# A state-space layer with a gated feed-forward: filter spectrum kept on chip with an exchanged copy, stages of two time steps, twiddles from a sine table, an explicit order

## The chip, the cores and the metric

The kernel runs on one core of a Trainium2 chip. A core has TensorE (matrix products, results into PSUM), VectorE (DVE), ScalarE (ACT), GpSimd (POOL) and SyncE (SP), which run side by side and meet at semaphores, and 16 DMA engines that move data between the memory off the core and SBUF. SP and ACT each have a queue from which they issue transfers; a queue issues in order, so an issue that waits holds up all that stand behind it. The metric is device time in microseconds, median of the runs.

## The reference

With S = 2048 time steps, D = 512 channels and F = 1792:

```python
xn = layernorm(A_q)                                     # over D
k_shift[t] = sum_j A_k[t - j] * shift_k[:, j]           # 4 taps
kv = k_shift * A_v
y  = irfft(rfft(kv, 2S) * rfft(ssm_k, 2S))[:S] + kv * ssm_D   # long convolution, per channel
s  = xn * y
h  = gelu(xn @ w_gate) * (xn @ w_up)
g  = silu(h @ w_down)
out = A_q + s * g
```

All inputs and the output are bfloat16. Two parts are independent until the end: the feed-forward (gate, up, down), and the long convolution, a product of two spectra of 4096 points.

## The kernel before

**Time steps.** A row of 128 partitions times 16: partition p holds time steps 16p to 16p + 15, and "row t" is the 128 steps with the same remainder t. `X` holds the input, `XN` the normalised input, `G` the gate and later the output, each 16 rows of 128 x 512.

**Feed-forward.** Four groups q of four rows. `ln(q)` (L857) takes statistics on DVE, a power on GpSimd and normalises on DVE; `xn_transpose(q)` (L882) brings channels to the partitions (`xnT`), by TensorE for q = 0 and by a DMA transpose on SP for the others. `unit(q, m)` (L1151) is one slice of 128 of the 1792 columns: four gate matmuls, four up matmuls of 512 columns, gelu on ACT (`GE`), product on DVE (`HT`). `down(q)` (L1178) is 14 matmuls a row, then tanh and a multiply into `G`, or silu in the last group.

**Convolution.** An FFT of two stages, each a matrix product, with the data regrouped through memory off the core between them.
- `h_transpose` (L917) turns the filter to time steps on the partitions (`HTr`) in 64 TensorE transposes of 128 x 128. `kshift` (L1026) computes the four taps on DVE into `V`.
- `stage1` (L999): row t against `F1[:, t]`, a table of cosines and sines that holds the first stage and the twiddle factors of row t together; two matmuls, one eviction of 128 x 1024 on ACT, one store of 256 KB to ZH (filter) or ZK (data). Filter evictions go to `ASH`, eight buffers inside `G`.
- `table` (L775), `phase`, `sins` make `F1`: 16 iotas on GpSimd, an addition and a mask on DVE, sines on ACT, each of 128 x 1024 in four parts. `G1`, its transpose, serves the last stage and is made by four DMA transposes (L1102). The second-stage matrices `MT` (three of 128 x 128) are made by some fifteen small operations (L960 to L989) and a sine, which needs ACT's table switched twice.
- `h_stage2(n)` (L1076), n = 0 to 7: loads 512 KB of ZH as `BH`, 16 matmuls on tiles of 32 x 32 (`tiles`, L1061; here a *set*), two evictions, and two stores of 256 KB to ZS.
- `spectrum(n)` (L1115): loads the filter spectrum from ZS into `HS` in two forms, so that real and imaginary parts stand at both places (two loads of 512 KB), loads `BK` from ZK, a forward set, two evictions to `KB`, four products on DVE into `HB` and `KS`, two inverse sets into one PSUM pair, two evictions to `BO` (two buffers), two stores to ZI, issued by ACT.
- At L1226 the last stage: 16 loads `BI` of 256 KB, four matmuls for two rows against `G1`, a multiply out of PSUM.

**Order.** `Sched.run` (L384) simulates the engines with assumed durations and picks, whenever an engine is free, the ready task of the lowest priority number (the `P_` constants) among those that could start within a small slack; PSUM banks and buffers are handed out on the way. Instructions are then issued in that order on each engine, and `Trk` puts in the semaphore waits. Input loads come first on SP, in the order of the string `ORDER`.

Of the kernel before, what the change touches and what calls it, by code (L numbers as in the profile page):

```python
# [14 lines left out]
DM = 512  # L15
# [8 lines left out]
N_WARM = 11  # L24
ORDER = ("w1 k0 v0 w2 k1 v1 w3 x1 d0 d1 k2 v2 k3 v3 x2 x3", "w1 k0 v0 w2 x1 k1 v1 w3 d0 d1 k2 v2 k3 v3 x2 x3",
         "w1 k0 v0 w2 k1 w3 v1 x1 d0 d1 k2 v2 x2 k3 v3 x3", "w1 k0 v0 w2 k1 v1 w3 d0 x1 d1 k2 v2 k3 v3 x2 x3")[int(0.2)]
NF_BANKS = 4
ISSUE = 470.0
NC_PAIRS = 4
SMALL = 1.15 * 262144  # L30
AHEAD = 2
T_FWD = 460.0
T_INV = 690.0
HS_FROM = int(13.29)
P_ZS = -25.414
P_HS = 40.705
P_BK = 2.723
P_XT = 19.554
P_G1 = -59.994
P_KB = 3.323  # L40
P_PI = -12.874
P_LN1 = 8.9
P_LN2 = 29
P_LN3 = 36.208
N_HOLD = 3
P_H1 = -137.134
P_K1 = 28.68
P_KSH = 10.596
P_KV = -81.664
P_BH = 0.174  # L50
P_H2 = 37.806
P_H2E = -118.293
P_K2 = -30.393
P_MUL = -44.647
P_BO = -10.624
P_ZI = -33.146
P_Q0 = 73.801
P_DN = 67.371
P_GE = 2.281
P_HT = 1.358  # L60
P_TA = 52.481
P_TG = -66.799
P_BI = 63.435
P_Y = 45.533
P_YD = -65.898
P_GX = 54.735
P_OD = 0.974
P_HTR = 0.191
P_SKB = 74.778
P_SG = 64.83  # L70
P_SU = 50.419
# [176 lines left out]
class Pool_:  # L248
# [26 lines left out]
    def find_all(self, n):  # L275

        got = []
        while len(got) < n:
            one = self.find()
            if one is None:  # L280
                break
            got.append(one)
            self.take(one[1])
        for f, i in got:
            self.used -= 1
            for j in range(i * self.size, (i + 1) * self.size):
                self.busy[j] = False
        return got if len(got) == n else None

# [25 lines left out]
class Task:  # L315
    __slots__ = ("n", "opts", "r", "w", "emit", "prio", "deps", "lat", "nbytes", "start", "end", "eng", "nleft", "outs", "heavy")


class Sched:


    SLACK = 105.145
    SEM = 90.0
    DMA_LAT = 2500.0
    LOAD_LAT = 1600.0
    HEDGE = 180.685
    DMA_BW = 370.0
    SHARE_BW = 130.0
    LOAD_BW = 313.0
    LOAD_BW0 = 240.0  # L330
    FIRST = {"loads": 900.0}
    QUEUE = {"ACT": 943.835, "DVE": 5.13899e+08}
    URGENT = 0.1
    DEFER = 51593

    def __init__(self):
        self.tasks = []
        self.n_loaded = 0

    def add(self, opts, emit, r=(), w=(), prio=5, lat=0.0, nbytes=0, after=(), heavy=None):  # L340
        t = Task()
        t.n = len(self.tasks)
        t.opts = [(e, max(d, nbytes / (self.LOAD_BW if self.n_loaded > 2e6 else self.LOAD_BW0)) if e == "loads" else d) for e, d in opts]
        self.n_loaded += nbytes if opts[0][0] == "loads" else 0
        t.r, t.w = list(r), list(w)
        t.emit = emit
        t.prio = prio
# [3 lines left out]
        t.heavy = heavy  # L351
# [11 lines left out]
        t.outs = []  # L363
        t.nleft = len(t.deps)
        for d in t.deps:
            d.outs.append(t)
# [9 lines left out]
    def behind(self, t, others):  # L376

        for d in others:
            if d not in t.deps:
                t.deps.append(d)  # L380
                t.nleft += 1
                d.outs.append(t)

    def run(self):  # L384
        free = dict(self.FIRST)
        pipe = 0.0
        loaded = self.FIRST["loads"] + sum(t.opts[0][1] for t in self.tasks if t.opts[0][0] == "loads")
        ready = [t for t in self.tasks if t.nleft == 0]
        order = []
        while ready:  # L390
            cands = []
            for t in ready:
                base = 0.0
                for d in t.deps:
                    base = max(base, d.end + d.lat + (self.SEM if not d.nbytes or t.opts[0][0] != "PE" else 400.0 if d.eng == "loads" else self.HEDGE))
                ok = True
                wants = {}
                for b in t.w:
                    if b.pool is not None and b.slot is None:
                        wants[b.pool] = wants.get(b.pool, 0) + 1  # L400
                for pool, n in wants.items():
                    av = pool.find_all(n)
                    if av is None:
                        ok = False
                        break
                    base = max(base, max(f for f, _ in av) + self.SEM)
                if not ok:
                    continue
                es = [(max(base, free.get(e, 800.0)), max(base, free.get(e, 800.0)) + dur, e) for e, dur in t.opts]
                es.sort(key=lambda x: x[1])  # L410
                cands.append((es[0][0], t, es[0][2], es[0][1]))
            assert cands, "the schedule is stuck"
            by_eng = {}
            for c in cands:
                if c[2] not in by_eng or c[0] < by_eng[c[2]]:
                    by_eng[c[2]] = c[0]
            eng = min(by_eng, key=lambda e: (by_eng[e], e))
            lo = by_eng[eng]
            mine = [c for c in cands if c[2] == eng and c[0] <= lo + self.SLACK]

            late = {}
            if eng == "PE":
                for e in ("ACT", "DVE"):
                    f = free.get(e, 800.0)
                    q = max(f - lo, 0.0) + sum(c[3] - c[0] for c in cands if c[2] == e and c[1].prio <= self.URGENT and c[0] <= max(lo, f) + self.SLACK)
                    late[e] = q > self.QUEUE[e]
            st, t, _, en = min(mine, key=lambda c: (c[1].prio + (self.DEFER if late.get(c[1].heavy) else 0.0), c[0], c[1].n))
            t.start, t.eng = st, eng
            free[eng] = en
            t.end = en  # L430
            if eng == "loads":
                t.end += self.LOAD_LAT
            elif t.nbytes:
                pipe = max(pipe, en + self.DMA_LAT / 2) + t.nbytes / (self.DMA_BW if en > loaded else self.SHARE_BW)
                t.end = pipe + self.DMA_LAT / 2
            for b in t.w:
                if b.pool is not None and b.slot is None:
                    b.slot = b.pool.find()[1]
                    b.pool.take(b.slot)
            for b in set(t.r + t.w):  # L440
                b.left -= 1
                b.last_end = max(b.last_end, t.end + t.lat)
                if b.left == 0 and b.pool is not None:
                    b.pool.release(b.slot, b.last_end)
            ready.remove(t)
            order.append(t)
            for o in t.outs:
                o.nleft -= 1
                if o.nleft == 0:
                    ready.append(o)  # L450
        assert len(order) == len(self.tasks)
        return order
# [14 lines left out]
def build_kernel(nc, A_q, A_k, A_v, A_shift_k, A_ssm_k, A_ssm_D, B_w_gate, B_w_up, B_w_down, out):  # L467
    with ExitStack() as es0:
# [21 lines left out]
        HB = at("HB", [128, 4, 2, DM], BF16, place["at"])  # L490
        F1 = new("F1", [128, NT, 2, 128], BF16)
        G1 = new("G1", [128, NT, 2, 128], BF16)
        MT = new("MT", [128, 3, 128], BF16)
        ident = new("ident", [128, 128], BF16)
        COLS = new("COLS", [128, 8], FP32)
# [3 lines left out]
        CC = new("CC", [128, 2, 128], I16)  # L499
# [5 lines left out]
        AST = new("AST", [128, 3, 2, 512], BF16)  # L505
# [14 lines left out]
        HTr = at("HTr", [128, NT, DM], BF16, kk_at - 16384)  # L520
        IO = at("IO", [128, 2, NT, 128], I16, kac_at)
        skr_at = kac_at + 8192
        SKR = at("SKR", [128, DM * 4], BF16, skr_at)
        C32 = at("C32", [128, 128], I32, xnT_at + 0)
        K32 = at("K32", [128, 128], I32, xnT_at + 512)
        S32 = at("S32", [128, 128], I32, xnT_at + 2368)
        Q32 = at("Q32", [128, 16], I32, xnT_at + 1024)
        PHI = at("PHI", [128, 128], I16, xnT_at + 1088)
        MSK = at("MSK", [128, 128], I16, xnT_at + 1600)
        BH = at("BH", [128, 2, 4, DM], BF16, g_at + 8192)  # L530
        ASX = at("ASX", [128, 2, 2, DM], BF16, kk_at - 2048)
        ASH = at("ASH", [128, 8, 2, DM], BF16, g_at)
        place["at"] = kk_at + 2048
        HS = new("HS", [128, 2, 2, 4, DM], BF16)
        KB = new("KB", [128, 4, 2, DM], BF16)
        BO = new("BO", [128, 2, 2, DM], BF16)
        KS = new("KS", [128, 4, 2, DM], BF16)
        BK = new("BK", [128, 2, 4, DM], BF16)
        assert place["at"] <= top
        BI = at("BI", [128, 8, 2, DM], BF16, kk_at + 2048)  # L540
        ast = {"H": [ASH[:, j, :, :] for j in range(8)], "K": [AST[:, j, :, :] for j in range(3)] + [ASX[:, j, :, :] for j in range(2)]}

        ZH = nc.dram_tensor("ZH", [NG, 128, DM], BF16, kind="Internal")
        ZK = nc.dram_tensor("ZK", [NG, 128, DM], BF16, kind="Internal")
        ZS = nc.dram_tensor("ZS", [NG // 4, 128, 4, DM], BF16, kind="Internal")
# [22 lines left out]
        def twins(name, ap):  # L568

            a, b = res(name + "e", ap), res(name + "o", ap)  # L570
            a.ovl.remove(b)
            b.ovl.remove(a)
            return [a, b]
# [752 lines left out]
```

## Time and profile before

| what | value |
|---|---|
| runs | 205.21, 204.33, 202.83 us; median 204.33 |
| span of the profiled execution | 201.5 us; its own run time is not on the page, the median of the runs is 2.8 us above the span |
| TensorE | 190.2 us busy (94%), 1391 matmuls |
| DVE | 153.1 us (76%) |
| ACT | 131.2 us (65%) |
| GpSimd | 16.5 us (8%) |
| DMA | 57.52 MB, mean 285 GB/s |

The profile is one execution, recorded by the chip. Times are from the start of the span. A line of the chain or of the timeline has the start in us, the length in us, the engine, the line of the code, the tiles and the count. "SPq" is SP's sequencer issuing a transfer; the time from issue to landing is listed apart: 6.1 us for HS<-ZS, 6.0 for ZH<-ASH and BK<-ZK, 5.2 for BH<-ZH, 5.0 for BI<-ZI, 3.0 for ZI<-BO (medians). A matmul counts as busy until its modelled end, so a TensorE that is 94% busy may issue with small gaps.

### The profile page before, as it was taken

The numbers are of one execution on the slowest core, as the hardware profiler recorded it, in microseconds if no ns is written. First come the engines' busy times: TensorE is split into PE (matmuls) and PEld (weight loads), VectorE is DVE, ScalarE is ACT, GpSimd is POOL, SyncE is SP. The second block draws the span as 40 slices with busy tenths as digits, with TensorE's granted clock in tenths as the row PEclk, the third lists the DMA queues.
The fourth block names the chain that finished last, engine by engine and source line by source line (L and its number), as shares of the span: only waits on it lengthen the run. The fifth ranks groups of instructions, "written<-read, shape, count | busy, mean of one in ns | idle before, by whom it ended". The sixth has DMA issues, their size and how long they took to land.

```text
span 201.5 us, 3616 instructions
## 1 busy us (share of the span) xinstructions
PE 190.2 (94%) x1391; PEld 86.1 (43%) x1404; DVE 153.1 (76%) x252; ACT 131.2 (65%) x168; POOL 16.5 (8%) x40
## 2 busy tenths in 40 slices
PE   7688999999999999999998999899999999999992
PEld 2466444444444444444343343333443444444461
DVE  6999589889998989997865675664676671339994
ACT  2477766769677799979843876587888786141111
POOL 7295000030000000002100000000000000000000
PEclk9999999999999999999999999999999999999999
DMA  5999999999999778788899999989896423677934
GB/s 193 349 369 324 367 390 394 394 413 389 259 274 316 292 254 294 291 292 305 304 243 326 340 307 402 325 289 288 272 317 184 145 101 123 209 246 226 333 131 148
DMA packets 44455, 57.52 MB, mean 285 GB/s; under 512 B 12947, under 2 KB 32279, under 8 KB 43414
## 3 DMA queue, kind: packets, MB, share of 16 engines
q1 hardware_dynamic: 37638, 48.77, 74.5%
q10 hardware_dynamic: 6800, 8.52, 11.9%
q8 instruction: 11, 0.18, 0.3%
q14 instruction: 6, 0.05, 0.1%
HBM read 35.78 MB, written 18.87 MB: 271 GB/s over the span
## 4 chain that ended last, share of the span: by engine, by line
PE 69%; DMA 15%; ACT 7%; DVE 4%; issue 1%; POOL 1%; SPq 1%; ACTq 0%
PE psall L678 65%; DMA ZS<-AST 6%; DMA ZI<-BO 5%; PE psall L1067 4%; DMA BK<-ZK 3%; ACT AST L1083 2%; ACT BO L674 1%; DMA X<-in_A_q_dram 1%; DVE stats L861 1%; POOL mv L871 1%; ACT F L768 1%; ACT GE L1172 1%; DVE XN L874 1%; ACT L1172 1%; SPq L654 1%
## 5 line engine op out<-in xcount | busy, mean ns | idle before, releaser
L678 PE MATMUL psall<-xnT,Wg 128*128 128x512 bf16 (+1 forms) x232 | 55.1, 372 | 3.3 <-ACT xnT L674 1.7
L678 PE MATMUL psall<-xnT,Wu 128*128 128x512 bf16 (+1 forms) x232 | 56.1, 373 | 1.0 <-ACT BO L674 1.0
L1175 DVE TENSOR_TENSOR HT<-psall,GE 128x512 bf16<-128x512 f32 x56 | 38.1, 688 | 23.9 <-PE psall L678 15.2
L678 PE MATMUL psall<-Wd,HT 128*128 128x512 bf16 (+1 forms) x231 | 50.5, 366 | 0.3
L1172 ACT ACTIVATE GE<-psall 128x512 bf16<-128x512 f32 x56 | 33.0, 599 | 19.3 <-PE psall L678 16.1
L678 PEld LDWEIGHTS psall<-xnT,Wg 128*128 128x128 bf16 x232 | 22.1, 98 | 30.3 <-ACT xnT L674 2.3
L678 PEld LDWEIGHTS psall<-Wd,HT 128*128 128x128 bf16 x238 | 23.0, 98 | 25.4 <-issue 1.1
L678 PEld LDWEIGHTS psall<-xnT,Wu 128*128 128x128 bf16 x232 | 21.0, 98 | 28.1 <-issue 3.5
L674 ACT ACTIVATE BO<-psall 128x1024 bf16<-128x1024 f32 x16 | 16.5, 1029 | 6.1 <-DMA ZI<-BO 4.3
L1201 DVE SCALAR_TENSOR_TENSOR G<-G,psall 128x512 bf16<-128x512 bf16 x12 | 8.2, 687 | 13.8 <-ACT G L1199 13.8
L674 ACT ACTIVATE ASH<-psall 128x1024 bf16<-128x1024 f32 x16 | 16.1, 1018 | 1.5 <-PE psall L678 1.5
L674 ACT ACTIVATE KB<-psall 128x1024 bf16<-128x1024 f32 x16 | 16.0, 1026 | 1.6 <-PE psall L678 0.9
L1048 DVE TENSOR_TENSOR KTM<-KK,SKB 128x2048 bf16<-128x2048 bf16 x12 | 14.6, 1220 | 0.2
L1050 DVE TENSOR_TENSOR KAC<-KAC,KTM 128x2048 bf16<-128x2048 bf16 x12 | 14.6, 1217 | 0.1
L1134 DVE TENSOR_TENSOR HB<-KB,HS 128x1024 bf16<-128x1024 bf16 x16 | 11.0, 689 | 3.4 <-ACT KB L674 1.7
L871 POOL TENSOR_TENSOR mv<-mv,NHALF 128x4 f32<-128x4 f32 (+1 forms) x5 | 6.5, 1293 | 83.3 <-DVE mv L870 83.3
L1199 ACT ACTIVATE G<-psall 128x512 bf16<-128x512 f32 x12 | 7.1, 601 | 9.5 <-PE psall L678 9.4
L674 ACT ACTIVATE AST<-psall 128x1024 bf16<-128x1024 f32 x11 | 10.9, 1024 | 2.1 <-PE psall L678 1.8
L1207 ACT ACTIVATE G<-psall 128x512 bf16<-128x512 f32 (+1 forms) x5 | 2.6, 512 | 14.1 <-PE psall L678 14.1
L861 DVE BATCH_NORM_STATS2 stats<-X 128x6 f32<-128x512 bf16 x16 | 10.4, 673 | 0.8 <-DMA X<-in_A_q_dram 0.8
L1134 DVE TENSOR_TENSOR KS<-KB,HS 128x1024 bf16<-128x1024 bf16 x16 | 11.0, 684 | 0.0
L1083 ACT ACTIVATE AST<-psall 128x1024 bf16<-128x1024 f32 x9 | 8.9, 1022 | 2.4 <-DMA ZS<-AST 1.8
(78 smaller groups left out, 163.0 us busy)
## 6 DMA issues: line engine op xcount, KB each, us to landing
HS<-ZS SPq DMA_DIRECT2D x16, 512.0 KB, 6.1
ZH<-ASH ACTq DMA_DIRECT2D x16, 256.0 KB, 6.0
BH<-ZH SPq DMA_DIRECT2D x8, 512.0 KB, 5.2
BK<-ZK SPq DMA_DIRECT2D x8, 512.0 KB, 6.0
ZI<-BO ACTq DMA_DIRECT2D x16, 256.0 KB, 3.0
BI<-ZI SPq DMA_DIRECT2D x16, 256.0 KB, 5.0
ZK<-AST SPq DMA_DIRECT2D x11, 256.0 KB, 3.3
ZS<-AST SPq DMA_DIRECT2D x9, 256.0 KB, 5.0
```

The costliest lines, as they stand in the source:

```text
L674: return h.activation(o, i, ACTF.Copy)
L678: return h.matmul(o, lhsT=l, rhs=r, start=st, stop=sp)
L861: t_stats[t] = op([("DVE", 670.0)], lambda e, h, t=t: h.bn_stats(stats[:, t, :], X[:, t, :]), r=[bX[q][t % 4]], w=[bst[t]], rr=[R_X[t]], w ...
L871: t_pw = op([("POOL", 800.0)], lambda e, hd, ts=ts, n=n: hd.tensor_tensor(mv[:, ts, 3:4], mv[:, ts, 2:3], NHALF[:, 0:n, :], ALU.pow), r=[b ...
L1048: op([("DVE", dur)], lambda e, h, j=j, m=m: h.tensor_tensor(KTM[:, m.slot, :, :], kk(j), sk(j), ALU.mult), r=need + [bSKB[j], a], w=[m], r ...
L1050: op([("DVE", dur)], lambda e, h, m=m: h.tensor_tensor(KAC[:, a.slot, :, :], KAC[:, a.slot, :, :], KTM[:, m.slot, :, :], ALU.add), r=[m], ...
L1067: trk.op("PE", lambda h: h.matmul(ps(s, i)[b, :], lhsT=MT[a, k, a], rhs=data(col)[a, :], start=n < 16, stop=n >= len(todo) - 16, tile_posi ...
L1083: op([("ACT", act(1024))], lambda e, hd, p=p, a=a: hd.activation(ast["K"][a.slot].rearrange("p c d -> p (c d)"), ps(psl(p)), ACTF.Copy, sc ...
L1134: op([("DVE", dve(1024, 2))], lambda e, hd, h=h, k=k, o=o, T=T: hd.tensor_tensor(flat(T, o), flat(KB, kb[h]), flat(HS, hs, (k, 2 * h)), AL ...
L1172: op([("ACT", act(512))], lambda e, h: h.activation(GE[:, g.slot, :], bank(pg), ACTF.Gelu_apprx_tanh), r=[pg], w=[g], rr=lambda: R_bank(pg ...
L1175: op([("DVE", dve(512, 1))], lambda e, h: h.tensor_tensor(HT[:, q % 2, m, :], bank(pu), GE[:, g.slot, :], ALU.mult), r=[pu, g], w=[bHT[q][m]],
L1201: op([("DVE", dve(512, 1))], lambda e, h, g=g, pc=pc: h.scalar_tensor_tensor(out=g, in0=g, scalar=1.0, in1=pc(), op0=ALU.add, op1=ALU.mult ...
```

## The change

1. **Filter spectrum in SBUF.** ZS is gone. `h_stage2(n)` evicts straight into `HS` (three buffers of 512 KB), and SP copies it from SBUF to `HW` with even and odd partitions exchanged (two copies of 256 KB over 64 partitions each). `spectrum(n)` multiplies in place in `HS` and `HW`. Since a buffer is free only behind the inverse set that reads it, the filter's second stage is now spread between the inverse sets; `BO` has four buffers, `BK` three.
2. **Pairs of time steps.** `h_transpose` reads two neighbouring bfloat16 as one fp32, 32 transposes with an fp32 identity; `stage1` handles two rows per buffer and stores 512 KB at a time in pieces of 4 KB; for the filter the eviction sorts the pairs by reading PSUM at a step of two. `BI` loads are eight of 512 KB.
3. **Twiddles from a sine table.** `F1` and `G1` are one matrix of 128 x 2 x 128. The twiddles move to the second stage: `TF`, one 32 x 32 weight per tile and group, is built from a table `TAB` of 128 x 4 x 32 sines by three products of 128 x 1024 on GpSimd; `m_turn` (four ACT copies) arranges it for two DMA transposes into `MI`, the inverse weights.
4. **Parking.** Filter evictions of the first stage go to rows 8 to 15 of `XN` and `X`; groups 2 and 3 of the input are loaded when these stores are done.
5. **Explicit order.** The string `SEQ` lists every task by number; a trailing "b" takes the second engine of the task. Evictions of 128 x 1024 may go to ACT or DVE (`EV`); twelve go to DVE. Three filler matmuls of TensorE (`hold`) are dropped, warm-up matmuls are 10 instead of 11, the first weight chunk has two slices of columns instead of four.

```diff
-N_WARM = 11
+N_WARM = 10
+ORDER = "x00 x01 x02 x03 w0 w1 h0 h1 h2 h3 D0 w2 s0 k0 v0 x1 w3 k1 v1 d0 d1 k2 v2 k3 v3 x2 x3"
+SEQ = (
+    "2 0 10 3 7 15 4 8 11 1 14 67 65 16 17 69 66 5 9 68 73 22 6 71 70 23 18 74 72 12 19 48 49 77 35 24 20 78 76 30 25 83 21 26 31 75 50 51 82 52 79 "
...
     def run(self):
...
-            st, t, _, en = min(mine, key=lambda c: (c[1].prio + (self.DEFER if late.get(c[1].heavy) else 0.0), c[0], c[1].n))
+        for name in SEQ.split():
+            t = self.tasks[int(name.rstrip("b"))]
+            eng, dur = t.opts[name[-1] == "b"]
...
+        ast = {"H": [T[:, 4 * j:4 * j + 4, :].rearrange("p (r c) d -> p r c d", c=2) for T in (XN, X) for j in (2, 3)], "K": [AST[:, j, :, :, :] for j in range(2)] + [ASX[:]]}
...
+        def EV(n):
+            return [("ACT", act(n)), ("DVE", dve(n, 1))]
...
+        def f_mul():
+            for c, off in ((0, float(TURN // 4 + TURN // 2)), (1, 0.0)):
+                PO(lambda h, c=c, off=off: h.tensor_scalar(C32[:, c, :], K4[:], Q32[:, 0:1], off, ALU.mult, ALU.add), [R_Q0, R_K4], [R_C32])
...
+        def m_table(e):
+            for i in range(2):
+                a, b = TAB[:, i, :].unsqueeze(2).broadcast_to([128, NG, 32]), TAB[:, 2 + i:3 + i, :].broadcast_to([128, NG, 32])
+                PO(lambda h, i=i, a=a, b=b: h.tensor_tensor(TM[i][:], a, b, ALU.mult), [R_TAB], [R_TM[i]])
+            PO(lambda h: h.tensor_tensor(TF[:], TM[0][:], TM[1][:], ALU.add), R_TM, [R_MF])
...
+                        src = Hn[:, k, :].bitcast(FP32).rearrange("p (a t) -> p t a", t=NT // 2)[:, 4 * hf + j, :]
+                        trk.op("PE", lambda h, o=o, src=src: h.transpose(o, src, ident32[:]), r=[R_Hn[k], R_id32], w=R_bank(pp[hf]), accum=True)
...
+                    return copy(e, h, ast[x][a.slot][:, :, :, 256 * i:256 * i + 256], ps(psl(p)).rearrange("p (c d r) -> p r c d", c=2, r=2))
...
+                dst = bass.AP(Z, 4 * u * DM, [[32 * DM, 128], [DM, 4], [1, DM]])
...
-                def st(e, a=a, h=h):
-                    dma(e, ZS[n][:, 2 * h:2 * h + 2, :], ast["K"][a.slot], d_ast["K"][a.slot], [R_AST["K"][a.slot]], [R_Z["S"][2 * n + h]])
+            def swap(e):
+                for c in range(2):
+                    dma(e, HW[hw.slot][c::2, :, :], HS[hs.slot][1 - c::2, :, :], d_hw[hw.slot][c], R_HS[hs.slot], [rh[c] for rh in R_HW[hw.slot]])
...
-                    dma(e, HS[h::2, hs.slot, :, :, :].rearrange("p k c d -> p (k c d)"), src, d_hs[hs.slot][h], R_Z["S"][2 * n:2 * n + 2], [R_HS[hs.slot][h]])
...
+                    def mul(e, hd, h=h, b=b, T=T):
+                        o = T[b.slot][:, 2 * h:2 * h + 2, :].rearrange("p c d -> p (c d)")
+                        return hd.tensor_tensor(o, flat(KB, kb[h]), o, ALU.mult)
...
+                tiles(pi, [(lambda c, m=m: MI[:, m, n, 32 * c:32 * c + 32], lambda c, T=T, b=b: T[b.slot][:, c, :], [R_MI[m], *R_b])
+                           for m, T, b, R_b in ((0, HS, hs, R_HS[hs.slot]), (1, HW, hw, sum(R_HW[hw.slot], [])))])
```

In the order that results, TensorE's first filter set (`BH`) stands behind the first stage of the data (`V`), and the first `BK` set comes behind three `BH` sets; the last inverse set is followed by 56 full matmuls before the first `BI` product. SP issues one `BH`, two `BK`, the exchange of the first group and a third `BK` one behind another; the DMA transposes for groups 2 and 3 stand between the exchanges. DVE does the phase steps before the first layer norm, GpSimd the sine products before the tap copies.

## The prediction

> **What bounds the kernel now.** I read the slices of the span first, then the chain that ended last, then the groups by shape.
>
> ```profile
> PE   7688999999999999999998999899999999999992
> ...
> DVE  6999589889998989997865675664676671339994
> ACT  2477766769677799979843876587888786141111
> ...
> DMA  5999999999999778788899999989896423677934
> ```
>
> TensorE shows 9 tenths in nearly every slice, DMA until 130 us too. A busy TensorE need not stream at its best pace, so I look for that pace in the chain.
>
> ```profile
> 18.14 1.47 PE psall L678 x8
> ...
> 30.46 10.74 PE psall L678 x49
> ...
> 87.83 5.04 DMA ZS<-AST
> ...
> 96.19 6.88 DMA ZS<-AST
> ...
> 105.88 5.31 DMA BK<-ZK
> ...
> 111.32 0.44 PE psall L1067 x16
> ...
> 118.40 9.21 DMA ZI<-BO
> ...
> 191.27 5.93 PE psall L678 x38
> ```
>
> The chain is TensorE from 18.14 to 86.3, transfers until 111.3, again at 118.4, and TensorE to 197.2. The piece at 30.46 plus its 0.05 us of issue is 10.79 us; the page counts 1391 matmuls to 1404 weight loads, so I take 50 matmuls, not 49: 0.2158 us each. With that TensorE's work sums to: 738 matmuls of 512 columns (432 gate and up, 210 down, 96 first and last FFT stages), 159.3 us; 60 of 256 columns at half, 6.5; 16 forward sets of 16 tiles at 0.365 (chain pieces 0.36 and 0.37) and 8 inverse sets at 0.58, 10.5; 64 transposes of the filter at 0.072 (4.6 us in all) and 16 of the input, 6.0. That is **182.3 us** of 201.5. Clock time minus the work of the instructions ahead (by their order) gives what was lost: 8.6 us at 18.14, 9.7 at 69.70 (first filter set), 11.7 at 111.32 (first BK set), 15.0 at 155.44, and 14.9 at 197.2. Behind that lies a tail of 4.3 us (silu, multiply, add, store). So 201.5 = 182.3 + 9.7 until 70 us + 5.2 from there + 4.3. The change can gain only from the 19.2 us that are not work.
>
> **The work itself.** Both orders hold the same matmuls, except that the filter is transposed as 32 pairs of bfloat16, read as one fp32, instead of 64 blocks. No fp32 transpose is in the trace: 0.072 us each if only the shape counts (2.3 us saved), 0.2158 if it costs the dearest single matmul of the trace (2.3 lost). I take 0.144, twice the bytes: 4.6 us, no change.
>
> **Until 70 us.** In the order of the new program, DVE does the phase steps ahead of the layer norm, and they wait for GpSimd: the iotas and two 128x128 multiplies at 0.86 and 0.77 (nearest rows, L978 and L977) from 0.8 us end at about 3.4. Then about 1.1 us of small DVE steps (0.15 to 0.36 by the like rows), so the first statistics start at 4.6 instead of 3.64. Four statistics at 0.66 with their small steps and two powers at 1.07 put the fourth normalised row at 11.1 instead of 12.0, but the second at 9.1 instead of 7.5. First gate matmul: about 11.3 instead of 9.53. Thereafter TensorE has a queue without the old holes: the gelu table is loaded once before any eviction (old: a load at 16.20, 1.28 us, that TensorE waited behind), the four phase additions on DVE (0.70 + 0.48 each) and four sines (1.15 each) are gone, and the first weight slice is half as large. At 13 us I get 12.95 on the clock against 5.05 of work: 7.9 us lost. After that ACT is tight: from 11.4 to 49.5 us it has 16 stage evictions at 1.02, 3 of the filter at 1.02, 12 gelus at 0.60, 4 half ones at 0.39, 8 store issues at 0.33 and some 4 us more, 35 of 38 us. I add 0.4: **8.3 instead of 9.7**.
>
> GpSimd's three 128x1024 fp32 products are not in the trace: 1.4 us each by length from the 128x512 copy (L1024, 0.69), 2.8 with two operands read in turn. I take the middle, 6.3 in all. They precede the next power and the tap copies; the tap row lands near 21 anyway, so 2 us more cost nothing, and at 2.8 each the cover is just used up. Late input rows 8 to 15 wait for the filter stores parked there (about 54 us); their layer norm comes at about 82, so 28 us hide it. SP issues the last weight load near 35, and xnT for group 1, up to 6.9 us of issue and 9.9 to land, arrives by 46 for use at 50. MI and G1 transposes together have 2304 columns instead of 4096 (7.44 us on SP at 51.49); the stores of K queued behind them wait less.
>
> **From 70 us.** Removed: 16 writes of 256 KB (ZS) and 16 reads of 512 KB (HS), 12.6 MB of 57.52. Added: 16 half exchanges of 256 KB, 4.2 MB. The exchange is not in the trace: 3.0 us (ZI<-BO, the fastest median of 256 KB) to 9.9 (the slowest transfer from SBUF to SBUF, xnT); I take 5.0. By the order, 12.5 us of work lie between the last forward filter set and its inverse, the narrowest of eight; evictions (2.1), exchange, four products (2.8) and the set (0.4) need 10.3, at 9.9 it would be 15.2, 2.7 late once. DVE now takes 12 of the 1024-wide evictions (1.22 each, 14.6 us) from ACT; its share there was 55 to 70%, so TensorE and ACT hide it.
>
> Of the 5.2 us, about 2 come from ACT waiting for ZS stores (the chain at 87.83 and 96.19) and 3.3 from 111 to 155, with BO waiting for its two buffers (ZI<-BO 9.21). ZS is gone and BO has four buffers. **What is late next is BK.** DVE's 32 tap products (1.22), 14 HT and 3 G in that stretch are 51 us from about 25, so the last K stage runs at 79.5, its stores are issued near 82, land 3.3 later (ZK median), and BK, issued behind them on SP, lands 5.31 after that: 90.8. TensorE reaches BK after 81.2 us of work, at 89.5: **1.3 lost**. With the shortest rows (2.4 and 4.8) nothing is lost, with the longest (7.5 and 7.5) 7.7. Behind that wait stand down projections in TensorE's order, and nothing else goes ahead. I leave 0.7 for the six stages behind it (old: 3.3). The last inverse set ends 12 us of work ahead of the first BI product; two evictions, ZI (4.9) and BI (5.0) fill that, so 0.3. The tail is unchanged.
>
> Sum: 182.3 + 8.3 + 2.3 + 4.3 = **197.2 us of span**. The median of the runs is 2.8 above the span shown, which I take for what lies around it: **200.0 us**, 2.1% below 204.33. By itself this forecast spans 197.5 to 202.5.
>
> **A rule against the change.** The first 11 matmuls took 0.43 us each, twice the later pace, though the row of the granted clock shows full speed. The old order has three filler matmuls at 7.75 between the transposes; the new one has none, and one warm-up matmul fewer, so from 5.4 to 11.3 us TensorE has only transposes and gaps. The mechanism would be that it falls back to the 0.43 pace and recovers after about the 4 us that the start took: 2 us more, 199.2 of span, 202.0. The Trainium skill, "TensorE: Matmul & The Clock Gate", says in its section "HAM oscillation" that idle gaps above about 3.4 us halve the clock, and in its "Part 4" that transposes do not count as busy in the same way. The trace agrees at the start (0.43 to 0.2158); it has no gap long enough to test the rest.
>
> **Rivals.**
> - *Half pace at the start*, as above: 202.0. For: no filler. Against: transposes stand in between. Chance 0.10.
> - *Slower: ACT becomes the bound of the filter stage.* The 16 stage evictions read PSUM at every second element to sort the pairs; the old ones read in line (1018 ns). A strided write (HTr) costs the same as a plain one (1.02), no strided fp32 read is in the trace. ACT has 3 us spare until 49.5, so it decides from 1.21 us each; at half rate (2.05) it costs 16.4 - 3 = 13.4: 210.6 of span, 213.4. At 1.6 each 6.3: 206.3. Chance 0.13.
> - *BK late at the long rows*: 7.7 instead of 1.3, 203.6 of span, 206.4; half of that 203.2. For: SP is one queue. Against: 8.4 MB fewer compete. Chance 0.12.
> - *Transfers hid anyway*: the order gives back what the traffic frees, lost time as before: 204. Chance 0.06.
> - *The order fits*: 0.5 us lost after 70 us and 7.5 ahead of it, 194.6 of span, 197.4. Chance 0.14.
> - *My sum*, 200.0: chance 0.45.
>
> **How the numbers follow.** The range reaches from 195.5 (the order fits, and cheap fp32 transposes) to 207.0 (BK at its long rows, strided evictions at 1.6); beyond it remain dear strided reads and several losses at once, under 0.2. About 1% (2 us) is what a measurement of this kernel can tell. Faster: my sum nearly all (0.43), the fitting order (0.14), half of the half-pace case (0.05), some of late BK (0.03): 0.65. Same: the rest of these and the hidden transfers, 0.17. Slower: strided evictions and late BK at its long rows, 0.18.
>
> **What would show it.** A first gate matmul at about 11.3 and 8.3 us lost by 70 us; stage evictions of ACT at 1.02; fp32 transposes at 0.144; last K stage near 80 and the first BK set at about 91, with a wait on DMA BK<-ZK of about 1.3; no wait of more than 1 us on the exchange; no stretch from 100 to 150 with more than 1 us lost; last matmul near 193. I am wrong if the order leaves TensorE waiting for ACT before 50 us, or for a transfer for more than 5 us in sum after it.

## The result, and the profile after

The changed kernel takes **217.3 us** (median; 217.28 to 217.48) against 204.4 for the kernel before (202.83 to 205.21): ratio 1.069, 95% interval 1.062 to 1.075. It is slower, and outside my range. The profiled execution took 217.29 us with a span of 215.5. Here and below, medians and ranges are those of all executions of a kernel, while a ratio compares only its undisturbed executions with undisturbed ones of the kernel before that ran beside it, so it is not always the quotient of the medians.

First the slices of the span, as the prediction showed them for the kernel before.

```profile
PE   0000789999999999999999999999999999999993
...
DVE  2000838999999988979888887788786680677984
ACT  3000098785686885787867587567658543440112
...
DMA  5999999897032689495799999596950322756255
```

A slice is 5.4 us. From the seventh to the last but one TensorE shows 9 tenths throughout. But in the first four, 21 us, it does nothing, and DVE and ACT nothing behind the first, while DMA runs at 9 tenths from the second on. The chain that ended last says for what they stand (start, length, what):

```profile
12.19 9.53 DMA KK<-AST
21.74 0.36 DVE PH L691
...
22.70 4.46 PE psall L601 x10
27.18 0.40 ACT TAB L702
27.60 1.28 ACT L706
...
32.47 1.03 PE psall L601 x8
...
100.55 0.37 PE psall L958 x16
...
109.80 0.44 PE psall L958 x16
...
200.54 11.11 PE psall L601 x62
```

`KK<-AST` is a transfer of 3 KB: zeros for the three rows of K ahead of the first time step. Behind it hang DVE's phase table `PH`, then TensorE's warm-up matmuls, then ACT's sines `TAB`. The view of waits (us in total, times, longest) has the same three:

```profile
ACT TAB L702 <- PE psall L601: 23.2, 1, 23.2
PE psall L601 <- DVE PH L693: 22.7, 1, 22.7
...
DVE PH L691 <- DMA KK<-AST: 18.3, 1, 18.3
```

**Why DVE waits for zeros.** `PH` and `TAB` lie in the stage buffer `AST[0]`, 1024 and 1536 bytes in. The first 1024 bytes of that buffer are the zeros (`ZERO`), which feed the warm-up matmuls and are the source of that transfer. The bytes do not overlap, but the kernel's tracker goes by records: the memset of the zeros, the warm-ups and the transfer are entered under `R_AST["K"][0]`, the record of the whole buffer, and the records of `PH` and `TAB` overlap it. A write waits for every earlier reader and writer of an overlapping record. So writing `PH` waits until the zeros have been read by the transfer; the warm-ups, which read zeros, wait for the writes of `PH`; and writing `TAB` waits for the warm-ups. The transfer is the 19th that SP issues, at 12.19 (in the kernel before it is the 16th), and it lands 9.53 us later, with 18 transfers issued ahead of it.

From 32.47 on almost nothing is lost. By the order of the instructions 176.8 us of work lie between that matmul and the end of the last at 211.64 (pace as in the prediction, 0.111 for an fp32 transpose); the clock shows 179.2.

### The profile page after: what moved, and what is told of

Same layout as the page of the kernel before. It is cut to its first block, busy times and chain, and to the rows that moved or that the text cites. A ratio compares the mean times of both kernels' runs of the same rounds, so it can differ in the third digit from the quotient of the medians.

```text
span 215.5 us, 3447 instructions
## 1 busy us (share of the span) xinstructions
PE 187.6 (87%) x1353; PEld 86.0 (40%) x1368; DVE 157.6 (73%) x244; ACT 119.5 (55%) x160; POOL 17.2 (8%) x29
## 4 chain that ended last, share of the span: by engine, by line
PE 85%; SPq 5%; DMA 4%; ACT 2%; issue 1%; DVE 1%
PE psall L601 79%; SPq L573 5%; PE psall L958 5%; DMA KK<-AST 4%; ACT HTr L592 1%; PE psall L857 1%; ACT L706 1%; DVE G L1105 0%; DVE G L1104 0%; ACT xnT L592 0%; ACT TAB L702 0%; ACT G L1102 0%; DVE PH L691 0%; DVE PH L692 0%; DVE PH L693 0%
## 5 line engine op out<-in xcount | busy, mean ns | idle before, releaser
L601 PE MATMUL psall<-Wd,HT 128*128 128x512 bf16 (+1 forms) x230 | 51.9, 367 | 0.5 <-issue 0.2
L1070 DVE TENSOR_TENSOR HT<-psall,GE 128x512 bf16<-128x512 f32 x54 | 36.8, 685 | 11.7 <-PE psall L601 11.4
L1067 ACT ACTIVATE GE<-psall 128x512 bf16<-128x512 f32 x54 | 31.0, 601 | 14.3 <-PE psall L601 12.8
L601 PE MATMUL psall<-AST 128*128 128x512 bf16 x10 | 4.4, 628 | 22.7 <-DVE PH L693 22.7
L592 ACT ACTIVATE HS<-psall 128x1024 bf16<-128x1024 f32 x15 | 14.8, 1022 | 3.5 <-PE psall L958 3.3
L592 ACT ACTIVATE BO<-psall 128x1024 bf16<-128x1024 f32 x11 | 11.0, 1022 | 8.5 <-PE psall L958 8.0
L592 ACT ACTIVATE KB<-psall 128x1024 bf16<-128x1024 f32 x11 | 10.9, 1023 | 6.0 <-PE psall L958 6.0
L691 DVE SCALAR_TENSOR_TENSOR PH<-ARR,Q,OFF 128x128 int32<-128x128 int32 x1 | 0.4, 353 | 18.3 <-DMA KK<-AST 18.3
L592 ACT ACTIVATE AST<-psall 128x1024 bf16<-128x1024 f32 x11 | 11.1, 1024 | 3.4 <-PE psall L601 3.1
L809 POOL TENSOR_TENSOR mv<-mv,NHALF 128x4 f32<-128x4 f32 (+1 forms) x5 | 4.9, 986 | 97.8 <-DVE mv L808 97.8
L601 PEld LDWEIGHTS psall<-AST 128*128 128x128 bf16 x10 | 1.3, 140 | 24.9 <-DVE PH L693 22.7
```

Of the source, the lines that this page charges most:

```text
L592: return h.activation(o, i, ACTF.Copy, scale=scale)
L601: return h.matmul(o, lhsT=l, rhs=r, start=st, stop=sp)
L809: t_pw = op([("POOL", 850.0)], lambda e, hd, ts=ts, n=n: hd.tensor_tensor(mv[:, ts, 3:4], mv[:, ts, 2:3], NHALF[:, 0:n, :], ALU.pow), r=[b ...
L1067: op([("ACT", act(512))], lambda e, h: h.activation(GE[:, g.slot, :], bank(pg), ACTF.Gelu_apprx_tanh), r=[pg], w=[g], rr=lambda: R_bank(pg ...
L1070: op([("DVE", dve(512, 1))], lambda e, h: h.tensor_tensor(HT[:, q % 2, m, :], bank(pu), GE[:, g.slot, :], ALU.mult), r=[pu, g], w=[bHT[q][m]],
```

## The experiments

The theory at first: **A**, the 20 us are this false wait and nothing else. The rivals: **B**, an early start collides with the loads; **C**, the TensorE clock falls without fillers.

### 1. Take the wait away (e1_named)

```diff
-        ZERO = AST[:, 0, 0, 0, :]
+        ZERO, R_zero = AST[:, 0, 0, 0, :], res("ZERO", AST[:, 0, 0, 0, :])
...
-                trk.op("PE", lambda h: mm(h, bank(warm), ZERO[:, 0:128], ZERO, True, True), r=[R_AST["K"][0]], w=R_bank(warm), accum=True)
+                trk.op("PE", lambda h: mm(h, bank(warm), ZERO[:, 0:128], ZERO, True, True), r=[R_zero], w=R_bank(warm), accum=True)
```

The memset and the transfer name `R_zero` likewise. Nothing else moves.

> The changed kernel; only the tracker's record of the zero row is narrowed to the 1 KB that is read, so the phase table beside it no longer counts as an overlap. Theory A, one false wait: the phase step starts near 3.5 us instead of 21.74, the warm-up matmuls near 1.2 instead of 22.70, the first gate matmul near 12 instead of 32.47, and the rest keeps its pace: span about 195, time about 197. Theory B, the wait had only hidden the rest of the change, since the loads ran 18 us ahead of the compute: after 30 us TensorE loses 5 to 8 us to loads, ACT or the BK round: time 202 to 206. Theory C, half pace at the start without filler matmuls: 199.

Measured: **209.07 us** (208.28 to 209.97), ratio 1.029 (1.014 to 1.044). The first gate matmul came at 11.77 as A said, 18 us sooner than in the changed kernel (29.80), but only 8.2 us came off the time. B was right in kind, though the time is above its 202 to 206. What took the rest stands first among TensorE's waits:

```profile
PE psall L601 <- DMA xnT<-XN: 8.8, 1, 8.8
```

`xnT<-XN` is the transposing copy that brings the second quarter of the input to the partitions. SP's queue (start, length of the issue) and the chain show it issued at 38.82, right behind the last loads, and landing 21.08 later:

```profile
24.57 6.24 SPq L573 DMA_DIRECT2D Wd<-in_B_w_down_dram  x2
30.85 6.76 SPq L573 DMA_DIRECT2D KK<-in_A_k_dram  x2
37.65 1.12 SPq L573 DMA_DIRECT2D V<-in_A_v_dram  x2
38.82 11.97 SPq L825 DMA_TRANSPOSE xnT<-XN  x1
```

```profile
38.82 21.08 DMA xnT<-XN
60.03 7.28 PE psall L601 x25
```

In the changed kernel the same copy was issued at 41.34, with the loads nearly through, and landed 8.4 later, at 49.7 (not 51.7, as an expectation below has it); TensorE, 18 us late, first read it at 69.95. **The first wait covered the second.** In the kernel before, the copy left at 46.98 and TensorE turned to the second quarter at 57.45, behind more of the first quarter's down projection; the new order turns to it at 51.

Part of the 209 is also the clock. Windows of two us (columns: window, length, busy time of PE, PEld, DVE, ACT, POOL with counts, granted clock, DMA share, GB/s):

```profile
6.00:8.00 2.00, 0.10 (x1) 0.13 (x2) 1.93 (x10) 0.36 (x2) 1.08 (x2) 1.00 1.00 357
8.00:10.00 2.00, 2.00 (x18) 1.99 (x19) 1.73 (x2) 1.38 (x2) 2.00 (x2) 0.73 1.10 352
10.00:12.00 2.00, 2.00 (x14) 1.87 (x13) 2.00 (x4) 1.58 (x2) 2.00 (x2) 0.50 0.99 346
...
58.00:60.00 2.00, 0.00 (x0) 0.00 (x0) 0.00 (x0) 0.00 (x0) 0.00 (x0) 0.50 0.98 353
60.00:62.00 2.00, 1.97 (x5) 0.72 (x6) 0.00 (x0) 0.00 (x0) 0.00 (x0) 0.50 0.19 22
```

The clock halves after TensorE has stood, and the 25 matmuls behind the wait took 7.28 us instead of 5.4.

### 2. The same wait shorter, longer, and in the kernel before

e2_kz_first issues the zeros fifth on SP instead of 19th (the expectation says sixteenth, their place in the kernel before); e3_kz_late issues them behind the down weights. Both keep the coarse record. e4_before_wait is the kernel before, with its phase table `C32` moved beside the zeros in the stage buffer, and no other edit:

```diff
-        C32 = at("C32", [128, 128], I32, xnT_at + 0)
+        C32 = at("C32", [128, 128], I32, ast_at + 1024)
```

> The changed kernel with the wait left in; only the load of the zero rows (KK from AST) is issued fifth on SP, directly behind the four input rows, instead of sixteenth. Theory A: the phase step waits until this load lands, near 6 us, so the time falls by about 14 to 16 us, to 201 to 204. If the wait were on something else than this load, the time stays at 217.

> The changed kernel with the wait left in; the load of the zero rows is issued behind the down weights, near 29 us instead of 12.2. Theory A: the phase step starts when it lands, near 38 to 40 us, and the whole end moves with it: 217 + 16 to 18 = 233 to 235. If the start is held by anything else, no change.

> The kernel before, with one change: its first phase product (C32) is placed in the second KB of the buffer whose first KB holds the zeros, as the changed kernel places its phase table. The tracker then makes DVE wait for the load of the zero rows, which SP issues at 8.36 us in the kernel before, with 3.5 us for the issue. Theory A: DVE's third operation starts when it lands, near 15 to 18 us, and the kernel before gets slower by 12 to 16 us, to 216 to 220. If such a wait can be made up later, below 208.

Measured, one execution each: **209.62**, **233.63** and **221.77** us, beside 204.3 for the kernel before. The profile pages of e3_kz_late and e4_before_wait have the wait (`C` is `C32`; behind the last bar stands the idle time of DVE ahead of the instruction, and what ended it):

```profile
L692 DVE SCALAR_TENSOR_TENSOR PH<-ARR,Q,OFF 128x128 int32<-128x128 int32 x1 | 0.4, 351 | 34.1 <-DMA KK<-AST 34.1
```

```profile
L746 DVE TENSOR_SCALAR C<-K,Q 128x128 int32<-128x128 int32 x1 | 0.3, 288 | 18.3 <-DMA KK<-AST 18.3
```

With the zeros late, all of the delay comes through: `DVE PH` waited 34.1 us instead of 18.3, 15.8 more, and the time rose by 16.3. The kernel before pays 17.5 for a wait of 18.3, somewhat more than the 216 to 220 that I expected for it. So the false wait costs about its full length as long as it is the longest. With the zeros early, the wait for them shrinks to 1.0 us, and the 7.4 us for `xnT<-XN` appear, as in experiment 1. A's figure fell in e2_kz_first, its mechanism stood in the other two.

### 3. The second wait: move the copy in the queue, or do without it

The new theory **F**: the copy stands in SP's queue behind loads that are needed later than it. Rival B: the loads are late as a whole, and another wait follows. All but e7_pe_late hold the narrow record of experiment 1. e5_loads issues three of the loads (the last quarters of K and V, and the third of V) behind the copy:

```diff
+        late = [S.tasks[n] for n in (44, 43, 45)]
+        order = [t for t in order if t not in late]
+        at_xt = order.index(xt_tasks[0]) + 1
+        order[at_xt:at_xt] = late
```

e6_pe turns the quarter on TensorE: 16 transposes near 27 us, two evictions. e7_pe_late does that to the changed kernel as it is, false wait and all. e8_pe_warm is e6_pe with `N_WARM = 16` instead of 10.

> The changed kernel with the narrow record of the zero rows (as in e1_named), and three of the half-megabyte loads that SyncE issued ahead of the transposing copy of the second quarter (the last two quarters of V and the last of K) issued behind it. Theory F (the second wait is a place in SyncE's queue: the copy starts only when the loads in front of it are through): in e1_named the copy was issued at 38.8 and landed at 59.9, TensorE stood 8.8 us for it; with 1.5 MB less ahead, at the 374 to 390 GB/s of that stretch, it lands about 4 us earlier, near 56, the wait is about 5 us, and the time 204 to 206 against 209.1. Theory B (the loads as a whole are late, whichever comes first): another wait, on K or V, takes its place and the time stays at 208 to 210.

> The changed kernel with the narrow record of the zero rows, and the second quarter turned on TensorE (16 bf16 transposes behind the matmuls of the stage near 25 us, two evictions of 1024, one on ACT and one on DVE) instead of by SyncE's copy. Theory F: the wait of 8.8 us and the slow pace after it (25 matmuls in 7.28 us instead of 5.4) go, 16 transposes at 0.11 come in: 207.5 - 8.8 - 1.9 + 1.8 = 198.6 us of span, a time of 200.4 (199 to 202). Theory B (something else of the loads is late too): 203 to 208.

> The changed kernel as it is, with its 20 us start behind the zero rows, and only the second quarter turned on TensorE. Theory F: there the copy landed at 51.7 and was first needed at 69.95, so its removal gives nothing and the 16 transposes cost 1.8: 217 to 220. If the copy costs anything of its own there, through the queue or the DMA engines that it takes from the loads, the time falls below 216.

> As e6_pe, with 16 instead of 10 warm-up matmuls. Theory C (the granted clock falls when TensorE stands for some microseconds): in e1_named TensorE was idle from 5.6 to 7.9 and the clock was 0.50 between 10 and 12 us, where 8 fp32 transposes took 1.71 us instead of 0.89 and 8 bf16 transposes 0.82 instead of 0.61; with warm-ups until 8.3 the clock stays at 1.00, 0.4 us is lost to their length and about 1.7 won: 1 to 1.5 us less than e6_pe. If the start is set by the loads and the normalization, no difference, or 0.4 more.

| kernel | us, median (range) | ratio (95% interval) | span, granted clock |
|---|---|---|---|
| e5_loads | 199.52 (198.24 to 200.28) | 0.988 (0.978 to 0.998) | 196.4, 1.000 |
| e6_pe | 200.50 (200.08 to 200.80) | 0.993 (0.988 to 0.997) | 198.7, 0.991 |
| e7_pe_late | 220.21, one | | 218.4, 0.997 |
| e8_pe_warm | 199.77 (199.74 to 200.43) | 0.987 (0.981 to 0.993) | 198.6, 1.000 |

F holds. e6_pe came out at its sum (198.6 forecast, 198.7 measured; the transposes took 0.91, and TensorE waited 0.8 for their eviction, where the sum had 1.8). In e7_pe_late the same edit gives nothing and costs 2.9, of which 0.9 is the zeros landing at 22.66 instead of 21.72: the second wait did not exist there. e7_pe_late and e6_pe differ only in the record of the zeros, and in neither does TensorE wait for the copy: 220.21 against 200.50. Freed of the second wait, the first alone is worth 19.7 us, which is A's 20. In e5_loads, with 1.5 MB less ahead of it, the copy was issued 3.4 us sooner and landed 14.3 later, at 49.7, in time; I had expected 56 and 204 to 206. The 4 us by which 1.5 MB less would bring the copy forward are less than half of the 10.2 that it gained. That moving the loads frees the copy is shown; whether it waited for its turn behind them or shared the DMA engines with them is not. No wait on K or V took its place, so B fell. The warm-ups keep the clock at 1.00 from 8 to 12 us, where e6_pe had 0.57, and bring 0.7 us, less than the 1 to 1.5 that C gave them.

### 4. What the first gate matmul waits for

In e1_named, e5_loads, e6_pe and e8_pe_warm the first two of the four normalizations took about 0.4 us each, the third 1.99 and the fourth 1.33. VectorE's instructions in e1_named:

```profile
7.80 0.41 DVE L812 TENSOR_SCALAR XN<-X,mv 128x512 bf16<-128x512 bf16 x1
8.48 1.99 DVE L812 TENSOR_SCALAR XN<-X,mv 128x512 bf16<-128x512 bf16 x1 [0.27 <-POOL mv L809]
...
11.06 1.33 DVE L812 TENSOR_SCALAR XN<-X,mv 128x512 bf16<-128x512 bf16 x1
```

and GpSimd's first two products, which run beside them:

```profile
8.42 3.82 POOL L698 TENSOR_TENSOR TM<-TAB 128x1024 f32<-128x1024 f32 x2
```

Theory **D**: the two do not run together. e9_warm is e5_loads with 16 warm-ups; e10_table adds a read of the four normalized rows to the products, so that they start behind them; e11_pe_table does the same to e8_pe_warm.

```diff
-                PO(lambda h, i=i, a=a, b=b: h.tensor_tensor(TM[i][:], a, b, ALU.mult), [R_TAB], [R_TM[i]])
+                PO(lambda h, i=i, a=a, b=b: h.tensor_tensor(TM[i][:], a, b, ALU.mult), [R_TAB, *R_XN[0:4]], [R_TM[i]])
```

> As e5_loads, with 16 warm-up matmuls instead of 10. In e5_loads' own profile TensorE was idle 1.3 us between 4 and 8 us and the clock stayed at 1.00 throughout, in e1_named and e6_pe it stood for 2.5 us and fell to 0.57 between 8 and 12: theory C (the dip is there in some executions, as the first slice of the filter lands sooner or later) expects the median to come to the level of e5_loads' best, 198.2 to 199, with less spread; without C nothing changes (199.5).

> As e9_warm, and GpSimd's three products of the phase table wait until the four row tiles of the first quarter are normalized. Theory D (a GpSimd product slows a VectorE instruction that runs beside it): in e1_named, e5_loads and e8_pe_warm the third of VectorE's normalizations began at 8.5, just behind the start of GpSimd's first product, and took 1.99 us, where others take 0.41; with the products behind them the four take about 0.4 each, the first gate matmul moves from 11.7 to about 10.3, and the time falls by 0.5 to 1.4 us against e9_warm (the second quarter, landed at 49.8 in e5_loads and needed at 50.7 there, may take some of it back). If the 1.99 has another cause (the clock, the loads), the instruction stays as long and the time as it is.

> As e8_pe_warm (the second quarter turned on TensorE, 16 warm-ups), and GpSimd's products behind the four normalizations as in e10_table. There the slow normalization fell from 1.99 to 0.41 us and the first gate matmul came at 10.6 instead of 11.7, but the 1.1 us were given back at the second quarter's copy (landed 54.5, waited for 3.6 us) and at a gate weight (1.0 us). With no copy to wait for, theory F leaves 0 to 1.1 of it: 198.7 to 199.8 against 199.8 for e8_pe_warm. If the order now runs against the loads in any case (the gate weight at 35 us, K's rows), the time stays at 199.8 or a little above.

| kernel | us, median (range) | ratio (95% interval) |
|---|---|---|
| e9_warm | 202.01 (199.35 to 203.01) | 0.980 (0.973 to 0.987) |
| e10_table | 203.11 (200.62 to 205.91) | 0.987 (0.981 to 0.994) |
| e11_pe_table | 199.29 (198.60 to 199.83) | 0.974 (0.970 to 0.979) |

D holds for the instruction. In e10_table:

```profile
8.47 0.41 DVE L812 TENSOR_SCALAR XN<-X,mv 128x512 bf16<-128x512 bf16 x1 [0.27 <-POOL mv L809]
...
9.48 0.40 DVE L812 TENSOR_SCALAR XN<-X,mv 128x512 bf16<-128x512 bf16 x1
```

The first gate matmul came at 10.44 instead of 11.19 in e9_warm, 0.75 sooner (the 1.1 of the last expectation is against e1_named), but the time did not fall. TensorE's waits in e10_table say where it went:

```profile
PE psall L601 <- DMA xnT<-XN: 3.6, 1, 3.6
...
PE psall L601 <- DMA Wg<-in_B_w_gate_dram: 1.0, 1, 1.0
```

An earlier TensorE only waits longer for the same copy, which landed 17.0 after its issue in e9_warm and 17.1 in e10_table, not 14.3 as in e5_loads' profile. In e5_loads the copy came 1.3 us ahead of its use (49.7 and 51.04); in e9_warm TensorE stood 2.2 us for it, and the granted clock was 0.83 in the mean from 50 to 60 us, as if halved for 3.4 us. That is the likely reason why e9_warm missed its expectation. It is not shown: the profiles of e9_warm and e10_table are of single executions above the median (202.84 and 203.99 us), the shorter ones left no trace, and why the copy lands sooner in one execution than in another I did not find out. With no copy to wait for, e11_pe_table came out 0.5 below e8_pe_warm, where the first gate matmul moved by 0.7 (11.20 to 10.50). The two were measured on different chips and e11_pe_table's own runs spread over 1.2 us, so this 0.5 is not clear of noise. e11_pe_table has the lowest median of all, by its ratio 2.6% below the kernel before, and TensorE waits for hardly anything:

```profile
PE   7999999999999999999999999999999999999993
```

## Why the prediction was wrong, point by point

**The step that failed: "Until 70 us".** It said that DVE's phase steps ahead of the layer norm "wait for GpSimd", and put the first statistics at 4.6. They wait for SP too. In the changed kernel the statistics began at 22.56 and 28.0 us were lost by 32.47, where I had 8.3 by 70. I asked which engine makes the operands of each moved step, and never which earlier readers of its *destination* it must wait for. The placement of `PH` and `TAB` was in the code, and the order of SP showed the zeros as the 19th transfer. With the wait taken away the statistics began at 4.33 and the first gate matmul came at 11.77, 11.20 and 11.19 (e1_named, e5_loads, e9_warm). My 4.6 was near. My 11.3 met 11.2 by luck: it had no GpSimd product that holds up the normalization, and without that collision the matmul came at 10.44 and 10.50 (e10_table, e11_pe_table).

**A second step failed, unseen in the result.** "xnT for group 1, up to 6.9 us of issue and 9.9 to land, arrives by 46 for use at 50." The use was right (51), the landing was not: 59.9 in e1_named. I took 9.9 from the kernel before, the slowest of its three copies; the copy of this group left there at 46.98, behind the loads, and took 8.5. Moved up into them, it took 21.1. I carried a transfer's duration to a place where the queue in front of it was another one.

**The rest of the sum held, in part because errors cancelled.** With both waits gone the profiled executions of e5_loads, e8_pe_warm and e11_pe_table have spans of 196.4, 198.6 and 196.8; I had 197.2. The medians, 199.3 to 199.8, are near the 200.0 that I gave to a kernel which did not exist. In e5_loads the last matmul ended at 192.6: 181.2 of work and 11.4 lost, where I had 182.3 and 10.6. About 10 of it were lost by the first filter set at 81.64 (71.1 of work by the matmuls in the trace, of which a few can be missing), where I had 8.3, and about 1 behind it, where I had 2.3. Term by term:
- fp32 transposes: 0.144 taken; 8 in 0.89 us in the chain of e5_loads, 0.111. 1.1 us less than I counted.
- Stage evictions that read every second element: 1032 and 1027 ns (`XN`, `X`), 1.02 taken. The dear strided read did not happen.
- The exchange `HW<-HS`: 5.0 taken, 4.3 median. The products that read it on DVE (`HW<-KB,HW`) waited 0.0 us.
- GpSimd's products: 6.3 taken, 3.82 and 2.35. Right in length; that they hold up the normalization beside them I had not asked.
- BK: 1.3 us of wait taken; 0.2 in e1_named, 0.6 in e8_pe_warm, none in e5_loads and e11_pe_table. First BK set "about 91": 90.7 in e5_loads, 91.1 in e11_pe_table, 92.9 in e8_pe_warm.
- From 100 to 150 us TensorE was busy 49.8 of 50 us in e5_loads and e11_pe_table: under 1 us lost, as said.
- Last matmul "near 193": it ended at 192.6 in e5_loads. Tail 4.3 taken; 3.9 in the changed kernel.
- What lies around the span: 2.8 taken from a median, 1.8 in the profiled run.

**The rivals.** None was the one that happened: the slower ones had their places behind 11 us, the cause lay before. The half pace at the start was real where TensorE stood ahead of the transposes: 0.57 of the clock from 8 to 12 us in e6_pe, worth the 0.7 us by which e8_pe_warm is faster, not my 2. (Of the first eleven matmuls of the kernel before, the last two were faster than the 0.43 us that I gave to all: their row is 4.20 us long.) The Trainium skill, "TensorE: Matmul & The Clock Gate", "HAM oscillation" and "Part 4: PE-mode transpose", puts the fall behind gaps of more than about 3.4 us and does not count transposes as busy in the same way. Where TensorE stood 2.3 and 2.5 us (e1_named, e6_pe, both from the last warm-up to the first transpose) the clock fell; where it stood 1.3 and 1.1 (e5_loads, e8_pe_warm) it did not, although e5_loads has only transposes from 6.92 to 11.20. In e9_warm a gap of 2.2 us between full matmuls was enough. So in these runs a gap shorter than the Trainium skill's 3.4 us halves the clock, and in e5_loads transposes behind a short gap kept it up.

## What to carry to other kernels

Before a moved instruction is priced, list what it waits for by its destination too: every earlier reader and writer of the record that covers those bytes, with the queue and the place in it of each, since a buffer shared with a slow 3 KB transfer cost 20 us here. A transfer's time belongs to its place in the queue and to the loads around it, not to the transfer alone: price it by what is issued ahead of it. And when one wait is removed and less than its length comes back, look for the next one on the same path; two waits that cover each other show in the profile only one at a time.

## What the runs showed of the hardware

- In e1_named a bfloat16 normalization on VectorE that began at 8.48, 0.06 us behind a GpSimd product of fp32, ended at 10.47, after 1.99 us; the next, at 11.06 beside the second product, took 1.33; with the products behind them, 0.41 and 0.40. The products ran from 8.42 to 12.24, 1.9 us each. In e2_kz_first and in the changed kernel a normalization began later beside the first product and took 0.76 and 0.44. All four ended 0.10 to 0.16 us behind the end of a product, however early they began; that is less than the 0.41 that one takes alone, which these rows do not explain. The Trainium skill, "SBUF — State Buffer", section "SBUF: two separate sides", describes an SBUF port pair that the two engines share and that the first to start holds for its whole instruction; these rows agree in that no normalization ended before the product beside it.
- A transposing copy of 512 KB from SBUF to SBUF landed 8.4 us after its issue behind nearly finished loads (the changed kernel), 14.3 to 17.1 with 1.5 MB less of loads ahead than in e1_named (e5_loads, e9_warm, e10_table), and 21.1 in e1_named, where the last loads of Wd, K and V had been issued in the 14 us before it.
- A TensorE transpose of 128 x 128 in fp32 takes 0.111 us in a row of eight (e5_loads), one in bfloat16 0.057 (16 in 0.91, e6_pe).
- The exchange of partitions from SBUF to SBUF, 256 KB a copy, landed in 4.3 us (median; 2.2 to 10.2) in the changed kernel, and TensorE did not wait for it.
